# Where two weight loads stand among GpSimd's casts, and how the last output block is cut

## The chip, the cores and the metric

The kernel runs on one core of a Trainium2 chip. A core has TensorE (PE), VectorE (DVE), ScalarE (ACT), GpSimd (POOL) and SyncE (SP), each with its own instruction queue in order, and sixteen DMA engines that all queues share. The metric is the device time of one execution in microseconds; the median of several runs counts.

## The reference

Sliding-window attention with a linear distance bias, then a feed-forward layer. B = 8 batches, H = 8 heads, S = 576 tokens, D = 64.

```python
scores = q @ k.T / 8 - slope[h] * |i - j|      # only 0 <= i - j < 128, else -1e9
attn   = softmax(scores) @ v                   # [B, H, S, D]
x      = attn.transpose(0, 2, 1, 3).reshape(4608, 512)
h      = x @ w_in                              # w_in  [512, 2048]
g      = h * clip(h + 3, 0, 6) / 6
out    = g @ w_out                             # w_out [2048, 512], out [4608, 512] fp32
```

## The kernel before

All matrix products are in bf16; q, k, v and the weights come as fp32. A group `g` is a pair of heads of one batch (NP = 4 groups in a batch, 32 in all); batch 0 is groups 0 to 3, batch 1 is groups 4 to 7. For each group PE forms the scores in two PSUM tiles, `scd` (the diagonal 128x128 blocks) and `sco` (the blocks beside the diagonal); ScalarE takes the exponential into `pd` and `po`; where no table was added to the scores, GpSimd masks them (lines 354 and 364). PE multiplies with v (`attend` in batches 0 and 1, `values` later; lines 383 and 391), DVE divides by the row sums, PE transposes the result (`back`, line 432), and it is copied into `xT`, the input of the feed-forward layer.

The feed-forward layer goes over nine blocks `nt` of 512 tokens. `moe_up(nt, ms)` is one of 16 steps for 128 columns of `w_in`: four matmuls (line 451), one activation on ScalarE (line 470), one multiplication on DVE (line 471). `moe_down(nt, step)` forms 128 rows of the output (`sub`) in four parts of four matmuls (line 483); at its end one engine copies the PSUM tile `ops` to `osb` and a DMA writes it out. For the last 128 rows of the last block, ScalarE copies the columns 0 to 255 and DVE the columns 256 to 511 of one PSUM tile, and two DMAs, on ScalarE's and on SP's queue, write 128 KB each. These units are woven between the attention steps by `fill(n)`, which takes the next `n` units of a fixed list as long as their tokens are ready. `up_begin(nt, ms, 3)` does the first three matmuls of a step ahead.

The order on every engine is the order in which the program is written: the whole kernel is in a manual schedule, so an instruction that waits holds all that stand behind it on its engine.

The weights are loaded by GpSimd's DMA queue, which casts them to bf16 on the way. `load_w_in(g)` loads the columns 512 g to 512 g + 511, so that the up steps `ms` = 4 g to 4 g + 3 need quarter g; quarter 0 is asked for earlier, between the casts of batch 0's v. `second_w_in` asks for quarter 1, with a memset ahead of it that touches one column of `w_out_sb`. `w_out_sb` serves in batch 0 as the room for `pd` and `po`, two rows of four for each of its four groups, and the touched place is the first of group 1's `pd`: the memset has to wait until PE has read it in `attend(1)`. `w_out` itself is loaded later, in `second_batch` (line 171).

q and k of batch 1 come over SP's queue into `ldbuf`, two pairs of heads at a time (`load_double`, two DMAs for each `dp` and each of k and q). `prepare_double(b, dp, copies, nms)` casts them to bf16 on GpSimd, two casts (line 227) for k and two for q; `wide_double` has PE transpose them (line 254). The v tokens of batch 1 follow on SP's queue as five DMAs (`load_tokens(1, "v")`, pieces of 256 bytes), then q and k of batch 2 (`load_double(2, ...)`). `cast_tokens(1, "v")` casts v on GpSimd (lines 187 and 190). Behind it on GpSimd stand two masks, the four loads of `w_out`, two masks, and the casts of batch 2's k and q, whose first result PE transposes at line 242.

The part of `first_batch` that the change touches:

```python
        prepare_double(1, 0, (P, P), early=second_w_in)   # between the first two casts
        ...
        prepare_double(1, 1, (P, P))
        load_w_in(2)
        load_w_in(3)
```

Of the kernel before, what the change touches and what calls it, by code (L numbers as in the profile page):

```python
# [10 lines left out]
FP32 = mybir.dt.float32  # L11
# [7 lines left out]
def kernel(  # L19
# [9 lines left out]
    nc = tc.nc  # L29
    B, H, S, D = q.shape  # L30
    d_model, d_ff = moe_w_in.shape
# [11 lines left out]
    n_ms = d_ff // 128  # L43
    n_ks = d_model // 128
    NT = 512
    n_nt = Ntok // NT
# [8 lines left out]
    w_out_sb = perm.tile([128, n_ms, d_model], BF16)  # L55
# [14 lines left out]
    opool = ctx.enter_context(tc.tile_pool(name="opool", bufs=4))  # L70
# [79 lines left out]
    def warm_up(n):  # L150
        w = ps_av.tile([128, 128], FP32, tag="av", name="w")
        for _ in range(n):
            nc.tensor.matmul(w, lhsT=ident, rhs=ident, start=True, stop=True)  # L153
# [11 lines left out]
    def load_w_in(g):  # L165
        nc.gpsimd.dma_start(
            out=w_in_sb[:, :, ts(g, 512)],
            in_=moe_w_in[:, ts(g, 512)].rearrange("(k p) f -> p k f", p=128))
# [6 lines left out]
    def second_w_in():  # L175
        nc.gpsimd.memset(w_out_sb[:, 4, 0:1], 0.0)
        load_w_in(1)
# [26 lines left out]
    def prepare(g, copies):  # L204
        for nm, copy in zip("qk", copies):
            pr = prs.tile([128, RT * D], BF16, tag=f"pr{nm}", name="pr",
                          padded_shape=[128, 2 * RT * D])
            copy(out=pr, in_=runs[nm][:, g % NP, :])
            st[g, nm] = pr

    def transposes(g, copies):
        b, hp = divmod(g, NP)
        for nm, dst, copy in (("q", qTb[b % 2], copies[0]), ("k", kTb[b % 2], copies[1])):
            src = st.pop((g, nm))
            tp = ps_h.tile([128, RT, RP], BF16, tag="h", name="tp", padded_shape=[128, 16, 64])
            for t in range(RT):
                for e in range(2):
                    r = slice(e * D, (e + 1) * D)
                    nc.tensor.transpose(tp[r, t, :], src[r, ts(t, D)], ident[r, r])  # L219
            copy(out=dst[:, hp, :, :].rearrange("p j c -> p (j c)")[:, 0:S].rearrange(  # L220
                "p (a t) -> p a t", t=RT), in_=tp.rearrange("p t a -> p a t"))

    def prepare_double(b, dp, copies, nms="kq", early=None):
        for nm, copy in zip(nms, copies):
            pr = prs.tile([128, RT, 2 * D], BF16, tag=f"pr{nm}", name="pr2")
            for e in range(2):
                copy(out=pr[:, :, ts(e, D)],  # L227
                     in_=ldbuf["qk".index(nm)][:, ds((2 * dp + e) * RT * D, RT * D)].rearrange(
                         "p (t d) -> p t d", t=RT))
                if early and (nm, e) == (nms[0], 0):  # L230
                    early()
            st[b, dp, nm] = pr

    BANKS = {"h": ps_h, "av": ps_av, "o": ps_o}
# [31 lines left out]
    def tables_diag(g):  # L266
        scd = ps_sc.tile([128, 2, 512], FP32, tag="sc", name="scd")
        st[g, "scd"] = scd
        for e in range(2 if diag_tabled(g) else 0):
            t = tab[:, 2 * (g % NP) + e, 1:2, :]  # L270
            nc.tensor.matmul(scd[:, e, :].rearrange("p (j c) -> p j c", j=4), lhsT=ident,
                             rhs=t.to_broadcast([128, 4, 128]), start=True, stop=False)
# [12 lines left out]
    def scores_diag(g):  # L285
        rooms(g)
        b, hp = divmod(g, NP)
        qT, kT = qTb[b % 2][:, hp, :, :], kTb[b % 2][:, hp, :, :]
        first = not diag_tabled(g)
        if (g, "scd") not in st:  # L290
            tables_diag(g)
        scd = st[g, "scd"]
        for j in range(4):
            for e in range(2):
                r = slice(e * D, (e + 1) * D)
                nc.tensor.matmul(scd[:, e, ts(j, 128)], lhsT=kT[r, j, :],  # L296
                                 rhs=qT[r, j, :], start=first, stop=first or j == 3)

    def tables_off(g):
        hp = g % NP  # L300
        sco = ps_sc.tile([128, 2, 512], FP32, tag="sc", name="sco")
        st[g, "sco"] = sco
        if full(g):
            for e in range(2):
                h = 2 * hp + e
                t = tab[:, h, 0:1, :]
                nc.tensor.matmul(sco[:, e, 128:512].rearrange("p (j c) -> p j c", j=3),
                                 lhsT=ident, rhs=t.to_broadcast([128, 3, 128]),
                                 start=True, stop=False)
                nc.tensor.matmul(sco[:, e, 0:128].rearrange("p (s c) -> p s c", s=2),  # L310
                                 lhsT=ident, rhs=tab[:, h, :, 0:64], start=False, stop=False)
# [26 lines left out]
    def exp_full(g):  # L338
        for e in range(2):
            exp_diag(g, e)  # L340
        exp_off_full(g)
# [98 lines left out]
    gts, ops = {}, {}  # L440
# [21 lines left out]
    def moe_up(nt, ms):  # L462
        gts[nt] = gbuf[nt % 2]
        hps, n = begun.pop((nt, ms), (None, 0))
        if hps is None:
# [5 lines left out]
        nc.vector.scalar_tensor_tensor(out=gts[nt][:, ms, :], in0=r6, scalar=1.0, in1=hps,  # L471
                                       op0=ALU.min, op1=ALU.mult)

    def moe_down(nt, step):
        sub, part = divmod(step, 4)
        if part == 0:
            if nt == n_nt - 1 and sub in (1, 2) or nt == 1 and sub == 0:
                ops[nt, sub] = ps_h.tile([128, d_model], FP32, tag="h", name="ops")
            else:
                ops[nt, sub] = ps_o.tile([128, d_model], FP32, tag="o", name="ops")  # L480
        for i in range(4):
            ms = part * 4 + i
            nc.tensor.matmul(ops[nt, sub], lhsT=gts[nt][:, ms, ts(sub, 128)],  # L483
                             rhs=w_out_sb[:, ms, :], start=(ms == 0), stop=(ms == n_ms - 1))
        if part == 3:
            rows = ds(nt * NT + sub * 128, 128)
            osb = opool.tile([128, d_model], FP32, tag="osb", name="osb")
            if nt == n_nt - 1 and sub == 3:
                nc.scalar.copy(out=osb[:, 0:256], in_=ops[nt, sub][:, 0:256])
                nc.vector.tensor_copy(out=osb[:, 256:512], in_=ops[nt, sub][:, 256:512])  # L490
                nc.scalar.dma_start(out=out[rows, 0:256], in_=osb[:, 0:256])
                nc.sync.dma_start(out=out[rows, 256:512], in_=osb[:, 256:512])
                return
            if nt == n_nt - 1 and sub % 2 == 0:
                nc.scalar.copy(out=osb, in_=ops[nt, sub])
                nc.scalar.dma_start(out=out[rows, :], in_=osb)
            else:
                nc.vector.tensor_copy(out=osb, in_=ops[nt, sub])  # L498
                nc.sync.dma_start(out=out[rows, :], in_=osb)
# [21 lines left out]
    V, P, A = nc.vector.tensor_copy, nc.gpsimd.tensor_copy, nc.scalar.copy  # L521
# [24 lines left out]
    def first_batch():  # L546
        prepare(0, (V, A))
        warm_up(20)
        tables_diag(0)
        tables_off(0)  # L550
        warm_up(10)
        transposes(0, (V, A))
        scores_diag(0)
        prepare(1, (P, V))
        transposes(1, (V, V))
        scores_off(0)
        exp_full(0)
        scores_diag(1)
        prepare(2, (P, P))
        tables_off(1)  # L560
        transposes(2, (V, V))
        scores_off(1)
        exp_full(1)
        scores_diag(2)
        prepare(3, (P, V))
        tables_off(2)
        transposes(3, (V, V))
        scores_off(2)
        exp_full(2)
        scores_diag(3)  # L570
        scores_off(3)
        exp_full(3)
        cast_v(0, 0, V)
        cast_v(0, 1, P)
        load_w_in(0)
        cast_v(0, 2, V)
        cast_v(0, 3, V)
        cast_v(0, 4, P)
        for dp in range(2):
            for nm in "kq":  # L580
                load_double(1, dp, nm, nc.sync)
        load_tokens(1, "v")
        attend(0)
        attend(1)
        back(0)
        attend(2)
        back(1)
        prepare_double(1, 0, (P, P), early=second_w_in)
        attend(3)
        back(2)  # L590
        up_begin(0, 0, 3)
        back(3)
        wide_double(1, 0, "q", V)
        prepare_double(1, 1, (P, P))
        load_w_in(2)
        load_w_in(3)
        for dp in range(2):
            for nm in "kq":
                load_double(2, dp, nm, nc.sync)
        up_begin(0, 1, 3)  # L600
        done[0] = NP
        fill(1)
        wide_double(1, 0, "k", A)
        fill(2)
# [147 lines left out]
```

## Time and profile before

| | |
|---|---|
| median of 3 runs | 324.28 us (324.0 to 325.56) |
| the profiled execution | 324.27 us, span 322.6 us |
| granted TensorE clock | 0.999 |
| PE busy | 311.8 us, 97% of the span |
| ACT, DVE, POOL busy | 61%, 54%, 43% |
| up-projection matmuls (line 451) | 640 instructions, 144.9 us |
| down-projection matmuls (line 483) | 576 instructions, 141.3 us |
| loads of `w_in` | 4 issues, 7.1 to 9.9 us to landing |

The span runs from the first to the last instruction; the execution's own time is 1.67 us longer. Matmuls are pipelined and their ends are modelled, so the starts of neighbouring matmuls tell more than their durations. A line of the timeline or the waits names the engine, the source line, the tile written and the tile read. "q0" is the DMA queue that GpSimd fills, "q1" that of SP.

### The profile page before, as it was taken

How to read it: one execution, taken by the hardware profiler on the slowest of the kernel's cores; microseconds unless marked ns; L12 is line 12 of the kernel's file. 1: busy time of each engine (PE TensorE's matmuls, PEld its weight loads, DVE VectorE, ACT ScalarE, POOL GpSimd, SP SyncE). 2: the span in 40 equal slices, each digit the busy share in tenths (PEclk: the TensorE clock that was granted, in tenths of full speed). 3: DMA queues.
4: the chain of work that ended last, by engine and by line, in shares of the span. 5: the costliest groups of instructions: out<-in, count | busy, mean ns of one | idle time of the engine just before them, and what ended most of it. 6: DMA issues, size and time to landing. Idle time of an engine off the chain costs nothing.

```text
span 322.6 us, 7017 instructions
## 1 busy us (share of the span) xinstructions
PE 311.8 (97%) x2722; PEld 166.1 (52%) x2722; DVE 173.1 (54%) x338; ACT 195.2 (61%) x334; POOL 140.1 (43%) x249
## 2 busy tenths in 40 slices
PE   7889999999999999999999999999999999999995
PEld 6565465554554454555677654455444444444442
DVE  6767574554356555555555555555556455455500
ACT  4749976877777666766676667666764344244301
POOL 7465592693593767356745665463331000000000
PEclk9999999999999999999999999999999999999999
DMA  7999999999999999999999999932112100000111
GB/s 279 223 323 201 273 243 201 231 232 200 202 255 177 219 214 184 200 223 205 187 191 200 225 190 199 220 84 79 26 50 84 56 34 35 33 33 33 67 65 65
DMA packets 131425, 51.90 MB, mean 161 GB/s; under 512 B 118976, under 2 KB 123328, under 8 KB 131392
## 3 DMA queue, kind: packets, MB, share of 16 engines
q1 hardware_dynamic: 126160, 45.43, 65.7%
q0 software_dynamic: 4224, 4.19, 8.2%
q10 hardware_dynamic: 1008, 1.84, 1.5%
q8 instruction: 21, 0.34, 0.4%
q14 instruction: 12, 0.10, 0.1%
HBM read 36.70 MB, written 9.44 MB: 143 GB/s over the span
## 4 chain that ended last, share of the span: by engine, by line
PE 82%; DMA 7%; ACT 4%; DVE 2%; POOL 2%; issue 1%; POOLq 0%
PE ops L483 37%; PE hps L451 33%; DMA ldbuf<-in_q_dram 3%; PE scd L296 3%; DMA qTb<-tbuf 2%; DMA w_in_sb<-in_moe_w_in_dram 2%; PE av L391 2%; PE av L383 2%; ACT r L470 2%; PE sco L328 1%; PE w L153 1%; ACT kTb L244 1%; DVE kTb L220 1%; PE tp L219 1%; POOL tbuf L194 1%
## 5 line engine op out<-in xcount | busy, mean ns | idle before, releaser
L471 DVE SCALAR_TENSOR_TENSOR gbuf<-r,hps 128x512 bf16<-128x512 f32 x144 | 98.7, 687 | 103.1 <-ACT r L470 101.6
L470 ACT ACTIVATE r<-hps,bias 128x512 f32<-128x512 f32 x144 | 99.0, 689 | 90.1 <-PE hps L451 89.7
L451 PE MATMUL hps<-xT,w_in_sb 128*128 128x512 bf16 (+1 forms) x640 | 144.9, 358 | 1.3 <-DMA w_in_sb<-in_moe_w_in_dram 0.4
L483 PE MATMUL ops<-w_out_sb,gbuf 128*128 128x512 bf16 x576 | 141.3, 379 | 0.0
L451 PEld LDWEIGHTS <-w_in_sb 128*128 128x128 bf16 x640 | 58.9, 98 | 54.7 <-DMA w_in_sb<-in_moe_w_in_dram 1.4
L483 PEld LDWEIGHTS <-gbuf 128*128 128x128 bf16 x576 | 53.8, 98 | 59.1
L354 POOL TENSOR_SCALAR_AFFINE_SELECT pd<-pd 128x512 bf16<-128x512 bf16 x48 | 29.5, 631 | 34.6 <-ACT pd L351 34.6
L364 POOL TENSOR_SCALAR_AFFINE_SELECT po<-po 128x512 bf16<-128x512 bf16 x48 | 30.1, 632 | 32.2 <-ACT po L361 32.1
L351 ACT ACTIVATE pd<-scd,bias_d 128x512 bf16<-128x512 f32 x48 | 31.5, 684 | 5.0 <-PE scd L296 3.6
L194 POOL CAST tbuf<-ldbuf 128x512 bf16<-128x512 f32 (+1 forms) x45 | 25.5, 611 | 18.7 <-DMA qTb<-tbuf 10.4
L498 DVE COPY osb<-ops 128x512 f32<-128x512 f32 x33 | 22.7, 687 | 20.3 <-PE ops L483 20.3
L361 ACT ACTIVATE po<-sco,bias_o 128x512 bf16<-128x512 f32 x48 | 33.0, 688 | 0.0
L402 DVE TENSOR_TENSOR avs<-av,rc 128x384 bf16<-128x384 f32 (+1 forms) x48 | 23.6, 491 | 1.6
L391 PEld LDWEIGHTS <-pd 128*128 128x128 bf16 x192 | 14.4, 97 | 8.3 <-POOL tbuf L194 0.5
L383 PE MATMUL av<-vbuf,po 128*128 128x65 bf16 x192 | 18.1, 193 | 0.5 <-POOL po L364 0.5
L391 PE MATMUL av<-vbuf,pd 128*128 128x65 bf16 x192 | 17.6, 194 | 0.3 <-ACT kTb L244 0.3
L187 POOL CAST vbuf<-ldbuf 128x1024 bf16<-128x1024 f32 x14 | 14.3, 1041 | 4.5 <-DMA ldbuf<-in_v_dram 4.5
L383 PEld LDWEIGHTS <-po 128*128 128x128 bf16 x192 | 14.4, 98 | 3.7 <-POOL po L364 0.7
L367 ACT ACTIVATE p4buf<-sco,bias_d 128x64 bf16<-128x64 f32 x48 | 15.5, 323 | 0.0
L227 POOL CAST pr<-ldbuf 128x576 bf16<-128x576 f32 x20 | 12.8, 667 | 4.1 <-DMA ldbuf<-in_q_dram 2.1
L296 PE MATMUL scd<-qTb,kTb 64*128 64x128 bf16 x256 | 12.7, 219 | 1.7 <-DVE kTb L220 0.9
L296 PEld LDWEIGHTS <-kTb 64*128 64x128 bf16 x256 | 7.2, 94 | 13.4 <-issue 9.7
(94 smaller groups left out, 208.9 us busy)
## 6 DMA issues: line engine op xcount, KB each, us to landing
out_dram<-osb SPq DMA_DIRECT2D x33, 256.0 KB, 2.4
ldbuf<-in_v_dram SPq DMA_DIRECT2D x32, 256.0 KB, 5.5
ldbuf<-in_q_dram SPq DMA_DIRECT2D x20, 256.0 KB, 4.8
ldbuf<-in_k_dram SPq DMA_DIRECT2D x16, 256.0 KB, 4.6
ldbuf<-in_q_dram SPq DMA_DIRECT2D x12, 288.0 KB, 7.2
ldbuf<-in_k_dram SPq DMA_DIRECT2D x12, 288.0 KB, 7.0
w_in_sb<-in_moe_w_in_dram POOLq DMA_DIRECT2D x4, 512.0 KB, 8.9
w_out_sb<-in_moe_w_out_dram POOLq DMA_DIRECT2D x4, 512.0 KB, 11.2
```

The source lines that it names most:

```text
L194: nc.gpsimd.tensor_copy(out=tbuf[:m, :, j, :], in_=s[:m, j, :, :].rearrange("p (i e) d -> p i (e d)", e=2))
L296: nc.tensor.matmul(scd[:, e, ts(j, 128)], lhsT=kT[r, j, :], rhs=qT[r, j, :], start=first, stop=first or j == 3)
L351: nc.scalar.activation(out=pd[:, e, :, :].rearrange("p j c -> p (j c)"), in_=sc[:, e, :], func=ACT.Exp, bias=bias_d[:, h:h + 1], scale=scale)
L354: nc.gpsimd.affine_select(out=pd[:, e, :, :], in_=pd[:, e, :, :], pattern=[[0, 4], [1, 128]], channel_multiplier=-1, base=0, compare_op=AL ...
L361: nc.scalar.activation(out=po[:, e, :, :].rearrange("p j c -> p (j c)"), in_=sc[:, e, :], func=ACT.Exp, bias=bias_o[:, h:h + 1], scale=scale)
L364: nc.gpsimd.affine_select(out=po[:, e, :, :], in_=po[:, e, :, :], pattern=[[0, 4], [-1, 128]], channel_multiplier=1, base=-1, compare_op=A ...
L383: nc.tensor.matmul(out_av, lhsT=po[:, e, qt % 4, :], rhs=vb[:, qt - 1, h, :], start=True, stop=False)
L391: nc.tensor.matmul(out_av, lhsT=d, rhs=vb[:, qt, h, :], start=(qt == 0), stop=True)
L451: nc.tensor.matmul(hps[:, lo:hi], lhsT=w_in_sb[:, ks, ts(ms, 128)], rhs=xT[:, ks, ds(src, hi - lo)], start=(ks == 0), stop=(ks == n_ks - 1))
L470: nc.scalar.activation(out=r6, in_=hps, func=ACT.Relu, bias=bias3[:, 0:1], scale=1.0 / 6.0)
L471: nc.vector.scalar_tensor_tensor(out=gts[nt][:, ms, :], in0=r6, scalar=1.0, in1=hps, op0=ALU.min, op1=ALU.mult)
L483: nc.tensor.matmul(ops[nt, sub], lhsT=gts[nt][:, ms, ts(sub, 128)], rhs=w_out_sb[:, ms, :], start=(ms == 0), stop=(ms == n_ms - 1))
```

## The change

Three edits.

The second quarter of `w_in` is asked for ahead of the first cast of batch 1's k, where before it stood between the first and the second cast. The third quarter is asked for between the two k casts and the two q casts of the second `prepare_double` of batch 1, where before it stood behind all four, together with the fourth; the fourth keeps its place.

The last 128 rows of the output are formed in two PSUM tiles, from different pools: first 16 matmuls of 384 columns, which ScalarE copies and sends out, then 16 matmuls of 128 columns with the same 16 stationary blocks loaded again, which DVE copies and SP sends out. Before there were 16 matmuls of 512 columns and the copies were cut at column 256.

```diff
+    def last_rows(nt, sub, cut=384):
+        rows = ds(nt * NT + sub * 128, 128)
+        osb = opool.tile([128, d_model], FP32, tag="osb", name="osb")
+        for lo, hi, tag, copy, eng in ((0, cut, "o", nc.scalar.copy, nc.scalar),
+                                       (cut, d_model, "h", nc.vector.tensor_copy, nc.sync)):
+            ps = BANKS[tag].tile([128, hi - lo], FP32, tag=tag, name="ops",
+                                 padded_shape=[128, d_model])
+            for ms in range(n_ms):
+                nc.tensor.matmul(ps, lhsT=gts[nt][:, ms, ts(sub, 128)],
+                                 rhs=w_out_sb[:, ms, lo:hi],
+                                 start=(ms == 0), stop=(ms == n_ms - 1))
+            copy(out=osb[:, lo:hi], in_=ps)
+            eng.dma_start(out=out[rows, lo:hi], in_=osb[:, lo:hi])
+
     def moe_down(nt, step):
         sub, part = divmod(step, 4)
+        if nt == n_nt - 1 and sub == 3:
+            if part == 3:
+                last_rows(nt, sub)
+            return
...
-            if nt == n_nt - 1 and sub == 3:
-                nc.scalar.copy(out=osb[:, 0:256], in_=ops[nt, sub][:, 0:256])
-                nc.vector.tensor_copy(out=osb[:, 256:512], in_=ops[nt, sub][:, 256:512])
-                nc.scalar.dma_start(out=out[rows, 0:256], in_=osb[:, 0:256])
-                nc.sync.dma_start(out=out[rows, 256:512], in_=osb[:, 256:512])
-                return
...
-        prepare_double(1, 0, (P, P), early=second_w_in)
+        second_w_in()
+        prepare_double(1, 0, (P, P))
...
-        prepare_double(1, 1, (P, P))
+        prepare_double(1, 1, (P,), "k")
         load_w_in(2)
+        prepare_double(1, 1, (P,), "q")
         load_w_in(3)
```

## The prediction

> **What bounds the kernel now.** I read the page first, then who waits for whom on PE, then the timelines of POOL and PE, the DMA windows and the last microseconds.
>
> ```profile
> PE 311.8 (97%) x2722; PEld 166.1 (52%) x2722; DVE 173.1 (54%) x338; ACT 195.2 (61%) x334; POOL 140.1 (43%) x249
> PE 82%; DMA 7%; ACT 4%; DVE 2%; POOL 2%; issue 1%; POOLq 0%
> ```
>
> PE is busy for 97% of the span and is 82% of the chain that ended last. So a change that moves loads and copies can only win the few places where PE stands still. The waits of PE between 20 and 60 us, where the weights come in:
>
> ```profile
> PE hps L451 <- DMA w_in_sb<-in_moe_w_in_dram: 0.4, 1, 0.4
> PE tb L432 <- ACT xT L438: 0.4, 2, 0.2
> PE hps L451 <- DVE gbuf L471: 0.3, 1, 0.3
> ```
>
> One matmul waits for `w_in` at all, for 0.4 us. The chain shows which, and POOL's timeline shows why:
>
> ```profile
> 26.59 0.61 POOL pr L227
> 27.21 7.12 DMA w_in_sb<-in_moe_w_in_dram
> 34.38 1.05 PE hps L451 x4
> ```
>
> ```profile
> 16.76 0.67 POOL L227 CAST pr<-ldbuf 128x576 bf16<-128x576 f32 x1
> 17.78 0.10 POOL L176 MEMSET w_out_sb<- 128x1 bf16 x1 [0.35 <-PE wide L391]
> 17.82 0.74 POOL L166 DMA_DIRECT2D w_in_sb<-in_moe_w_in_dram  x1
> 19.69 0.66 POOL L227 CAST pr<-ldbuf 128x576 bf16<-128x576 f32 x1 [1.14 <-DMA ldbuf<-in_k_dram]
> 23.57 0.67 POOL L227 CAST pr<-ldbuf 128x576 bf16<-128x576 f32 x1 [0.57 <-DMA ldbuf<-in_k_dram]
> 25.10 0.67 POOL L227 CAST pr<-ldbuf 128x576 bf16<-128x576 f32 x1 [0.87 <-DMA ldbuf<-in_q_dram]
> 27.21 1.48 POOL L166 DMA_DIRECT2D w_in_sb<-in_moe_w_in_dram  x2
> ```
>
> Columns: start, duration, line, operation, and in brackets POOL's idle time before it with its releaser. The third and fourth quarter are issued at 27.21 and 27.95, behind a cast that waited for a q load. The third lands 7.1 us later, at 34.33, and up-projection step 8 starts at 34.38.
>
> **Part 1, the second quarter ahead of the first cast: nothing.** In the row above POOL had already finished the first cast (16.76 + 0.67 = 17.43) and stood idle for 0.35 us: the memset waits for PE's line 391, the first matmul of `attend(1)`, which reads the part of `w_out_sb` that the memset touches. It started at 17.52 and is not moved. So memset and issue stay at 17.78 and 17.82, whoever is queued behind them. The cast now comes after the issue: 17.82 + 0.74 = 18.56, and ends near 19.23. The next cast cannot start before its k data at 19.69, which leaves a cover of 0.46 us. Without that cover a late cast would push the three after it, and PE's transposes of q at 22.50 follow the last one (ending 22.18) by 0.3 us. PE's step 4, the first to read this quarter, started at 27.72; its PSUM buffer was freed by DVE (line 471) only at 27.67, so even an earlier landing would have been worth at most 0.05 us. I take 0.
>
> **Part 2, the third quarter between the casts of k and q.** The last k cast ends at 23.57 + 0.67 = 24.24. The issue takes 0.74 and ends at 24.98; the q cast behind it starts at 25.10 because its load lands then, so 0.12 us of cover remain. If that went, q's casts (ending 27.26) would be late by tenths; PE takes this q at 30.33, 3 us later. The fourth quarter keeps its place at 27.21. POOL's mask (line 354) behind it may start 0.7 us sooner, which is worth nothing: PE reads that tile in `attend(4)` at 41.33.
>
> When does the third quarter land? From issue to landing the four quarters took 8.0, 9.9, 7.1 and 9.8 us, so 24.24 gives 31.3 to 34.1. In the DMA windows the second quarter's packets run until about 26.4, then POOL's queue is nearly empty until 29.4. The third can use that hole. Landing by 31.5 is my value.
>
> What does PE gain? Step 8 could start as soon as the score matmuls before it are through: they start at 33.57 and the same group took 0.29 us elsewhere (29.17 to 29.46), so 33.86 instead of 34.38, 0.52 us. ScalarE takes the result; it had been idle for 0.46 us before its step at 35.45, and is then busy without a gap until 42.7. So 0.46 us is what can be passed on. I take 0.46, bounds 0 and 0.52.
>
> What does the hole cost others? It was not empty: the v tokens of batch 1, on SP's queue, ran in it alone. Each row is one microsecond (the first from 28, the pair from 30); packets, MB, share of 16 engines:
>
> ```profile
> q1 hardware_dynamic: 894, 0.23, 99.9%
> ```
>
> ```profile
> q0 software_dynamic: 164, 0.17, 103.1%
> q1 hardware_dynamic: 61, 0.02, 11.4%
> ```
>
> Beside `w_in` (q0) the v tokens (q1) fall from some 860 packets in a microsecond to between 60 and 240. They now lose the hole and get it back after 33.3 instead of 36.3, three microseconds sooner. The engines do the same work in another order, and the last v packets stay near 36.9. SP is held in its v issues meanwhile, and the q and k loads of batch 2 behind them start later; their casts begin at 44.98, some 7 us after those loads run. The last v landings gate POOL:
>
> ```profile
> 38.12 1.04 POOL L187 CAST vbuf<-ldbuf 128x1024 bf16<-128x1024 f32 x1 [3.78 <-DMA ldbuf<-in_v_dram]
> 44.98 2.50 POOL L227 CAST pr<-ldbuf 128x576 bf16<-128x576 f32 x4
> ```
>
> From 38.12 POOL has no gap until 49.94. The first two casts at 44.98 end at 46.26; PE transposes their result at 46.43. With PE 0.46 earlier it would want it at 45.97 and wait 0.29. A little behind, PE stood still for 0.36 us at 47.62 for ScalarE (line 438), whose chain is shifted too, so that wait is absorbed.
>
> **Part 3, the last block.** PE's last matmul ended at 318.82, and then:
>
> ```profile
> 318.85 0.37 ACT L489 COPY osb<-ops 128x256 f32<-128x256 f32 x1 [2.87 <-PE ops L483]
> 319.25 0.42 DVE L490 COPY osb<-ops 128x256 f32<-128x256 f32 x1 [6.62 <-ACT osb L489]
> 319.70 0.33 SPq L492 DMA_DIRECT2D out_dram<-osb  x1
> ```
>
> The two copies of one PSUM tile run one after the other: 0.88 us from PE's end to the last issue. Now there are two PSUM tiles, so DVE's copy waits for PE alone. The first copy (384 columns; between 0.37 for 256 and 0.585 for 512, so 0.48) and its issue run beside the short matmuls. DVE's copy of 128 columns: 0.687 for 512, 0.423 for 256, so 0.29. From PE's end: 0.03 + 0.29 + 0.03 = 0.35, saving 0.53. The last transfer halves to 64 KB; it landed in 1.8 us, and I count nothing for that (bound: 0.1 better).
>
> PE pays: 16 matmuls of 512 columns took 16 x 0.216 = 3.45. Those of 384 (line 307) are 0.16 to 0.17 apart: 16 x 0.163 = 2.61. Those of 128 with a weight load each (line 254) start at 23.87 nine at a time, and the next operation at 24.37, 0.056 each: 0.89. Sum 3.50, a loss of 0.05. Net gain 0.48, bounds 0.1 (were the short ones paced by their weight loads, 98 ns by line 483: 1.57 in place of 0.89, which eats 0.68 and turns it into a loss of 0.2) and 0.6. I take the row of line 254 because it has the same load and the same width; the loss of 0.2 stays in the range.
>
> The Trainium skill, TensorE: Matmul & The Clock Gate, section Back-to-back issue gap, speaks against this cut: it gives about 81 ns for each 128-column matmul in a stream of loads and matmuls, and 131 ns for one of 512 columns. By it the short ones would take 1.30 us and the gain of the last block would shrink to about 0.1. The trace has 56 and 216 ns.
>
> **The sum.** The profiled execution took 324.27 us (span 322.6 and 1.67 around it), 0.01 from the median of 324.28. 324.27 - 0 - 0.46 - 0.48 = 323.3. That is 0.3% less; 0.5% (1.62 us) is about what a measurement of this kernel can tell from no change, so the likeliest verdict is within.
>
> **Rivals.**
> - *Only the tail lands.* PE's 0.46 is taken back before 60 us, at the transposes of 46.43 or at the waits on ScalarE at 47.6 and 48.3. For it: POOL's chain from 38.12 is not moved by PE. Against: the 0.36 at 47.62. 324.27 - 0.48 = 323.8. Chance 0.17.
> - *The v tokens come late.* If the two quarters hold them back altogether until 33.3, the some 4,040 v packets left at 26.4 need 4.7 us from there, to 38.0 instead of 36.9. POOL's chain starts 1.1 later, PE waits for k at 46.43; all but 0.1 is paid: 324.3. The change is slower than before once v is later than about 1.0 us, and by over 0.5% from 2.6 us (SP's held issues leaving its queue empty would do it): 324.3 to 326. For it: 61 against 164 packets above. Against: work is only reordered. Chance 0.2, of it 0.14 beyond 0.5%.
> - *More comes free.* The hole near 29.4, where the engines idled 0.4 us, closes, v lands earlier and POOL's chain with it, and the gains stand at their upper bounds: 324.27 - 0.52 - 0.6 - 0.4 = 322.75; the scatter of the runs (324.0 to 325.56 before) decides whether it passes 0.5% (322.66). Chance 0.16, of it 0.12 beyond.
> - That part 1 does not do what it says is in the forecast.
>
> The forecast has 0.47. Scatter puts 0.03 of it past 0.5% faster and 0.01 of the tail's rival past 0.5% slower; so faster 0.15, slower 0.15, same 0.70. The range of eight in ten goes from 322.5 (half of the free gain's case lies below) to 325.0 (a little over half of the late v tokens' case above).
>
> **What would show it.** Right: memset still near 17.8 behind an idle POOL; third quarter issued near 24.3, no PE wait on `w_in` at step 8; v cast near 38; DVE's last copy 0.3 us behind PE's end. Wrong: the v cast past 39, PE waiting for POOL's casts near 46, or short matmuls at 80 ns and more.

## The result, and the profile after

The changed kernel's median is 323.47 us over 22 runs (322.6 to 325.71), that of the kernel before over the 22 runs beside them 325.13 us (324.0 to 327.75). The ratio is 0.996, with a 95% interval of 0.9944 to 0.9976: some 1.3 us faster, between 0.8 and 1.8. The profiled execution took 323.38 us, span 321.7.

The front on POOL (start, duration, line, operation, idle time before it and its releaser):

```profile
17.93 0.11 POOL L176 MEMSET w_out_sb<- 128x1 bf16 x1 [1.26 <-PE wide L391]
17.97 0.74 POOL L166 DMA_DIRECT2D w_in_sb<-in_moe_w_in_dram  x1
18.71 0.68 POOL L227 CAST pr<-ldbuf 128x576 bf16<-128x576 f32 x1
21.12 1.42 POOL L227 CAST pr<-ldbuf 128x576 bf16<-128x576 f32 x2 [1.74 <-DMA ldbuf<-in_k_dram]
26.41 0.74 POOL L166 DMA_DIRECT2D w_in_sb<-in_moe_w_in_dram  x1
28.48 0.67 POOL L227 CAST pr<-ldbuf 128x576 bf16<-128x576 f32 x1 [0.39 <-DMA ldbuf<-in_q_dram]
37.95 1.04 POOL L187 CAST vbuf<-ldbuf 128x1024 bf16<-128x1024 f32 x1 [2.94 <-DMA ldbuf<-in_v_dram]
```

The memset waits for line 391 as before. The third quarter is issued at 26.41, two microseconds ahead of the last q cast; both the k and the q data came one to two microseconds later in this execution than in the first trace. GpSimd casts v in three pieces; the second v cast, at 37.95, stands where it stood (38.12). PE around steps 4 to 9 of the up projection, in the changed kernel:

```profile
27.46 1.97 PE L451 MATMUL hps<-xT,w_in_sb 128*128 128x512 bf16 x7
31.93 1.90 PE L451 MATMUL hps<-xT,w_in_sb 128*128 128x512 bf16 x8
35.83 1.04 PE L451 MATMUL hps<-xT,w_in_sb 128*128 128x512 bf16 x4
```

and in the kernel before:

```profile
31.26 1.90 PE L451 MATMUL hps<-xT,w_in_sb 128*128 128x512 bf16 x8
34.38 1.04 PE L451 MATMUL hps<-xT,w_in_sb 128*128 128x512 bf16 x4 [0.45 <-DMA w_in_sb<-in_moe_w_in_dram]
35.68 1.04 PE L451 MATMUL hps<-xT,w_in_sb 128*128 128x512 bf16 x4
```

The 8 matmuls at 31.93 are steps 6 and 7, the 4 at 35.83 are step 9. Between their starts lie 3.90 us; before, from 31.26 to 35.68, 4.42. (I measure to step 9, since the record of step 8's first matmul is missing in several traces.) The wait for the third quarter is gone. The waits of PE between 20 and 60 us show one that is new:

```profile
PE hps L451 <- DMA w_in_sb<-in_moe_w_in_dram: 0.9, 1, 0.9
PE tb L432 <- ACT xT L438: 0.4, 2, 0.2
PE tp L254 <- POOL pr L227: 0.3, 1, 0.3
```

The 0.9 us stands at 22.37, at the first matmul of the up projection, which reads quarter 0. Its load is not touched by the change, and no other of the fourteen traces has this wait: it is this execution's. The end of the changed kernel, and below it the copy of the rows before (`sub` 2) in the kernel before:

```profile
315.12 0.58 ACT L507 COPY osb<-ops 128x512 f32<-128x512 f32 x1 [6.32 <-PE ops L501]
317.72 0.48 ACT L485 COPY osb<-ops 128x384 f32<-128x384 f32 x1 [2.01 <-PE ops L482]
318.61 0.29 DVE L485 COPY osb<-ops 128x128 f32<-128x128 f32 x1 [6.25 <-PE ops L482]
318.93 0.33 SPq L486 DMA_DIRECT2D out_dram<-osb  x1
```

```profile
315.39 0.58 ACT L495 COPY osb<-ops 128x512 f32<-128x512 f32 x1 [6.32 <-PE ops L483]
```

From the copy of `sub` 2 to the last issue: 318.93 - 315.12 = 3.81 us, before 319.70 - 315.39 = 4.31. DVE's copy now waits for PE, not for ScalarE.

**Two traces are not enough.** The spans differ by 0.9 us, and one could take it for the prediction's 0.94. Only 0.50 of it is in the tail. At the first output copy the changed kernel is 0.17 *later* (60.33 against 60.16), because of the 0.9 us at 22.37. Between the output copies at 101 and 111 us it wins 0.59 (9.54 against 10.13), where GpSimd waits for a DMA transpose that the change does not touch (4.76 us against 5.35). So the front's gain was neither shown nor refuted by this pair, and the experiments had to tell.

### The profile page after: what moved, and what is told of

Read it like the earlier page. It is cut to its first block, busy times and chain, and to the rows that moved or that the text cites. A ratio compares the mean times of both kernels' runs of the same rounds, so it can differ in the third digit from the quotient of the medians.

```text
span 321.7 us, 7010 instructions
## 1 busy us (share of the span) xinstructions
PE 308.1 (96%) x2699; PEld 166.7 (52%) x2738; DVE 172.7 (54%) x338; ACT 195.1 (61%) x334; POOL 140.7 (44%) x249
## 4 chain that ended last, share of the span: by engine, by line
PE 82%; DMA 5%; ACT 4%; POOL 4%; issue 2%; DVE 2%; SPq 1%; POOLq 0%
PE ops L501 35%; PE hps L451 35%; DMA ldbuf<-in_q_dram 3%; PE scd L296 2%; DMA qTb<-tbuf 2%; PE av L391 2%; PE av L383 2%; ACT r L470 2%; PE sco L328 1%; PE ops L482 1%; ACT kTb L244 1%; PE tp L254 1%; POOL tbuf L194 1%; ACT gbuf L351 1%; SPq L98 1%
## 5 line engine op out<-in xcount | busy, mean ns | idle before, releaser
L451 PE MATMUL hps<-xT,w_in_sb 128*128 128x512 bf16 (+1 forms) x621 | 142.7, 358 | 2.3 <-DMA w_in_sb<-in_moe_w_in_dram 0.9
L501 PE MATMUL ops<-w_out_sb,gbuf 128*128 128x512 bf16 x540 | 134.2, 380 | 2.3 <-issue 1.7
L501 PEld LDWEIGHTS <-gbuf 128*128 128x128 bf16 x560 | 52.2, 98 | 57.2
L354 POOL TENSOR_SCALAR_AFFINE_SELECT pd<-pd 128x512 bf16<-128x512 bf16 x48 | 29.6, 631 | 34.5 <-ACT pd L351 34.4
```

The source lines that it names most:

```text
L354: nc.gpsimd.affine_select(out=pd[:, e, :, :], in_=pd[:, e, :, :], pattern=[[0, 4], [1, 128]], channel_multiplier=-1, base=0, compare_op=AL ...
L451: nc.tensor.matmul(hps[:, lo:hi], lhsT=w_in_sb[:, ks, ts(ms, 128)], rhs=xT[:, ks, ds(src, hi - lo)], start=(ks == 0), stop=(ks == n_ks - 1))
```

## The experiments

All edits are relative to the kernel before or to the changed one; "old place" is that of the third quarter behind the q casts, "new place" that between k and q. Each traced kernel gave one more look at the front.

**Tail alone.** Both front edits undone:

```diff
-        second_w_in()
-        prepare_double(1, 0, (P, P))
+        prepare_double(1, 0, (P, P), early=second_w_in)
...
-        prepare_double(1, 1, (P,), "k")
-        load_w_in(2)
-        prepare_double(1, 1, (P,), "q")
+        prepare_double(1, 1, (P, P))
+        load_w_in(2)
         load_w_in(3)
```

> Only the cut of the last 128 output rows is changed. My theory: the tail is worth 0.48 us by itself, 0.15% (the same in every run, since nothing in it waits for a load): from the start of the copy of sub 2 to the issue of the last transfer 3.81 us as in the changed kernel, against 4.31 before; ratio 0.9985. Rival A (the front gives nothing and the whole measured 1.3 us is the tail): ratio 0.996. Rival B (the 128-column matmuls are paced by their weight loads): 32 matmuls take over 4.1 us and the ratio is 1.000 or above.

Measured: 0.9967 (0.9951 to 0.9983), 3.82 us from the copy of `sub` 2 to the last issue. The timing is about twice what the trace shows, so it was repeated:

> The tail-only kernel once more, because its timing (0.9967, 0.9951 to 0.9983) is about twice what its trace shows (0.50 us from the copy of sub 2 to the last issue, and some 0.1 us sooner landing: 0.9982). Theory: the trace is right, ratio 0.997 to 0.9985, and both timings together hold 0.9982. Rival (the tail gains a further 0.5 us that the trace does not show, after the last instruction): ratio 0.9967 again or below, with the execution's own time less than 1.6 us above the span.

Measured: 0.9976 (0.9957 to 0.9994); 3.81 us. Both intervals hold 0.9982. The last transfer, 64 KB, landed in 1.6 to 1.7 us where 128 KB took 1.8, so the trace accounts for some 0.6 us (0.50 and 0.1). Rival B falls: the 32 matmuls took 3.49 us, not over 4.1. Rival A (the whole gain is the tail, 0.996) is not excluded by the timing, since both intervals hold 0.996 too; their middles make the tail worth 1.1 and 0.8 us. But no row shows more than the 0.6: the second traced execution took 1.7 us more than its span, as the others did. Where the rest of that timing would come from stays open.

**Third quarter alone.**

```diff
-        prepare_double(1, 1, (P, P))
+        prepare_double(1, 1, (P,), "k")
         load_w_in(2)
+        prepare_double(1, 1, (P,), "q")
         load_w_in(3)
```

> Only the third quarter of w_in stands between the k and the q casts. My theory: this edit carries the rest of the gain: no wait of PE for w_in at up step 8, 0.46 us or somewhat more on average, because in single runs the third quarter comes later than in the one profiled; ratio 0.997 to 0.9985. Rival (the front gains nothing that lasts: what PE wins at step 8 is taken back before 60 us, and the 0.6 us that the changed kernel's profile won at 103 us, at a DMA transpose, was chance): ratio 1.000, and the first down-projection matmul of the kernel near 51.8 us as before.

Measured: 0.997 (0.9946 to 0.9995). Again:

> The third-quarter-only kernel once more. From step 6 to step 9 of the up projection the five traces with the old place of the third quarter took 4.42, 4.37, 5.54, 4.59 and 5.46 us, all eight with the new place 3.90. Theory: 3.90 again, the second v cast before 38.5 us (38.1 to 40.8 with the old place), and the edit alone is worth 0.5 to 1.2 us: ratio 0.996 to 0.9985. Rival (the front gains less than the tail and is lost in the scatter): ratio 0.999 to 1.001.

Measured: 0.9987 (0.9972 to 1.0002). Steps 6 to 9 took 3.90 and 3.91 us, the second v casts came at 38.02 and 37.51. In the first timing the edit gains by itself; the second interval just includes no change. Its size lies between 0 and 1.8 us by the two intervals, near 0.7 by their middle.

**Second quarter alone.**

```diff
-        prepare_double(1, 0, (P, P), early=second_w_in)
+        second_w_in()
+        prepare_double(1, 0, (P, P))
```

> Only the second quarter is asked for ahead of the first cast of batch 1's k. My theory: nothing, ratio 1.000 (0.998 to 1.002): the memset still waits for PE's first matmul of attend(1), starts near 17.8 to 17.9 with POOL idle for about 1.2 us before it, and the cast behind it still ends before its successor's data land. Rival (part 1 is what makes the changed kernel's front start without a wait at step 4): ratio 0.998 or below, with PE's step 4 free of a wait and the issue earlier than 17.8.

Measured: 1.0009 (0.999 to 1.0028). The memset started at 18.33, after POOL had been idle for 1.93 us. Its front has the old place of the third quarter, and PE pays for it:

```profile
32.33 1.90 PE L451 MATMUL hps<-xT,w_in_sb 128*128 128x512 bf16 x8
36.57 1.04 PE L451 MATMUL hps<-xT,w_in_sb 128*128 128x512 bf16 x4 [1.58 <-DMA w_in_sb<-in_moe_w_in_dram]
```

The wait that was 0.45 in the first trace is 1.58 here: the q casts ended late, and the third quarter was issued at 29.14 instead of 27.21. The v tokens were late as well, though not for the second v cast, which stands at 38.09, but for the third:

```profile
41.60 0.61 POOL L190 CAST vbuf<-ldbuf 64x512 bf16<-64x512 f32 x1 [2.47 <-DMA ldbuf<-in_v_dram]
```

**The changed kernel without part 1, and the changed kernel again.** In the first, `second_w_in` goes back between the two k casts:

```diff
-        second_w_in()
-        prepare_double(1, 0, (P, P))
+        prepare_double(1, 0, (P, P), early=second_w_in)
```

> The changed kernel with part 1 undone: the second quarter again between the two k casts, the third between k and q, the new tail. Theory 1 (part 1 is worth nothing or costs up to 0.3 us, the other two add up): ratio 0.994 to 0.996, at or below the changed kernel's repeat in this call; step 8 follows step 6 in 2.6 us without a wait for w_in. Theory 2 (part 1 helps where the k data come late, because the memset and the issue then no longer stand behind the cast: 18.9 and 19.4 us in the two kernels with the old order, 17.9 and 18.3 in those with the new one): PE waits 0.3 to 0.8 us at step 4 for the second quarter, and the ratio is 0.001 to 0.002 above the changed kernel's.

> The changed kernel once more, for the comparison on one chip and a second trace of it. Theory: ratio 0.995 to 0.997; no wait of PE of more than 0.2 us at step 8; 3.81 us from the copy of sub 2 to the last issue; from 101 to 111 us it takes about 9.5 us between the two output copies there, as in all traces but that of before (10.1), which would show that this 0.6 us is no part of the change. Rival (the 0.6 us at 103 us belongs to the change): traces without the third quarter's move show 10.1 there; the tail-only kernel already showed 9.7.

Measured on one chip: 0.9969 (0.9942 to 0.9995) without part 1, 0.9965 (0.9939 to 0.9991) with it. Part 1 is worth nothing that can be measured here. The wait of 0.3 to 0.8 us at step 4 that Theory 2 expected without part 1 is not in that trace. But Theory 2 has the mechanism half right. In the old order the first cast can wait for its k data, and then the memset stands behind it. POOL in the first third-quarter-alone trace:

```profile
18.76 0.67 POOL L227 CAST pr<-ldbuf 128x576 bf16<-128x576 f32 x1 [2.57 <-DMA ldbuf<-in_k_dram]
19.37 0.11 POOL L176 MEMSET w_out_sb<- 128x1 bf16 x1
```

There PE then waited 0.75 us for the second quarter at step 4. In the old order the memset started between 17.78 and 19.39 in seven traces; in the new one between 17.93 and 18.76 in six, with POOL idle for `attend(1)` each time. The edit takes away that late tail, but waits for the second quarter at step 4 remain: 0.62 and 0.75 us in two of the seven old ones (tail alone, third alone), 0.32 and 0.24 in two of the six new ones (second alone, third with second). It does not show in the time.

**No gate.** The changed kernel without the memset:

```diff
-        second_w_in()
+        load_w_in(1)
         prepare_double(1, 0, (P, P))
```

> The changed kernel, without the memset ahead of the second quarter, so that nothing holds its issue back but POOL's order. My theory: the memset is what sets the issue; without it the issue comes near 16.6, 1.3 us sooner, and the quarter's packets go among the k and q loads of batch 1. PE gains nothing from it, since in the kernel before step 4 was also held by DVE until 27.67; the k and q casts come later. Ratio to before 0.996 to 1.000, so the same as the changed kernel or up to 1 us worse. Rival (the gate costs time): ratio 0.993 or below.

Measured: 0.9977 (0.9953 to 1.0). The issue came at 16.14, step 4 had no wait for it, and PE waited 0.9 us for the casts of batch 1's k or q (line 254). The memset does set the issue. In this one trace the wait at step 4 is gone and one for a cast stands in its place, and the ratio is not better than that of the changed kernel.

**The third quarter with the second.**

```diff
         second_w_in()
+        load_w_in(2)
         prepare_double(1, 0, (P, P))
...
-        prepare_double(1, 1, (P,), "k")
-        load_w_in(2)
-        prepare_double(1, 1, (P,), "q")
+        prepare_double(1, 1, (P, P))
         load_w_in(3)
```

> The changed kernel with the third quarter asked for right behind the second, near 19.5 us, ahead of all casts of batch 1's k and q. It doubles what part 1 and part 2 could cost: 1 MB of weights between the loads of batch 1 and ahead of its v. Theory (step 8 has no wait any more, so an earlier third quarter brings nothing; the k and q loads already issued keep their order, v comes later): ratio 0.995 to 0.999, step 8 still 2.6 us behind step 6, the second v cast near 38 to 39 us. Rival (the late v tokens of the prediction): the v cast past 39 us, PE waiting for the casts near 46 us, ratio 0.999 to 1.003. Third possibility (even earlier is better): ratio 0.994 or below.

Measured: 0.9965 (0.9943 to 0.9987); steps 6 to 9 in 3.90 us, the second v cast at 38.29. With the third quarter asked for 4 to 7 us earlier than in the other kernels of the new place, the v tokens still were not past 39: the rival of late v tokens falls here too, and going earlier brings nothing beyond what the new place brings.

**The kernel before, against itself.**

> The kernel before once more, timed against itself. It tells what the comparison can tell: ratio 1.000 with an interval of about 0.002 on either side. Its second trace: theory (the 0.6 us lost near 103 us in the first trace was that execution's): 9.5 to 9.7 us between the output copies at 101 and 111 us; step 8 again waits for the third quarter, 0.4 to 1.6 us. Rival (the loss near 103 us belongs to the kernel before): 10.1 us again.

Measured: 1.001 (0.9989 to 1.0031). This trace was the surprise. The waits of PE between 20 and 60 us, and POOL's second v cast:

```profile
PE tp L242 <- POOL pr L227: 1.3, 1, 1.3
PE hps L451 <- DMA w_in_sb<-in_moe_w_in_dram: 0.8, 1, 0.8
```

```profile
40.60 1.04 POOL L187 CAST vbuf<-ldbuf 128x1024 bf16<-128x1024 f32 x1 [5.52 <-DMA ldbuf<-in_v_dram]
```

The mechanism that I feared from the change (v late, POOL's chain late, PE waiting at line 242 for batch 2's k) is here in the kernel *before*. Between 101 and 111 us it took 9.96, so my figure of 9.5 to 9.7 for this trace was wrong. The old place gave 9.39 to 10.13 there in five traces, the new one 9.28 to 9.69 in nine. Most of the 0.59 of the first pair was that pair's; whether a part of it belongs to the change stays open.

**All traces, by the place of the third quarter.**

| kernel | third issued | steps 6 to 9 | second v cast |
|---|---|---|---|
| old place: before | 27.21 | 4.42 | 38.12 |
| before again | 27.53 | 4.59 | 40.60 |
| second alone | 29.14 | 5.54 | 38.09 (third: 41.60) |
| tail alone | 28.32 | 4.37 | 39.17 |
| tail alone again | 28.64 | 5.46 | 40.78 |
| new place: changed | 26.41 | 3.90 | 37.95 |
| changed again | 24.39 | 3.90 | 37.36 |
| tail and third | 24.61 | 3.90 | 37.48 |
| third alone | 24.48 | 3.90 | 38.02 |
| third alone again | 24.03 | 3.91 | 37.51 |
| no gate | 26.86 | 3.90 | 37.67 |
| cut at 448, at 256 | 23.96, 24.39 | 3.90, 3.90 | 37.58, 38.23 |
| third with second | near 19.5 | 3.90 | 38.29 |

In all five traces the old place costs PE something at step 8: 0.47 to 1.64 us above 3.90, on average 0.98 (the sum of 0.52, 0.69, 1.64, 0.47 and 1.56, divided by five). In none of the nine did the new place. The second v cast comes at 39.35 on average in the old place and at 37.79 in the new; the third, the last, at 40.84 and 38.80.

**Does PE keep what it wins at step 8?** The first output copy, before and in the changed kernel:

```profile
60.16 0.68 DVE L498 COPY osb<-ops 128x512 f32<-128x512 f32 x1
60.33 0.69 DVE L510 COPY osb<-ops 128x512 f32<-128x512 f32 x1
```

From step 9 to this copy the two took 24.48 and 24.50 us. Thirteen of the fourteen traces lie between 24.48 and 24.55, whatever the place; only the second trace of the kernel before took 25.40, with its wait at line 242. So nothing of the gain is taken back before 60 us, and the rival "Only the tail lands" does not hold in the traces.

The mean of 0.98 is more than a typical execution loses, however. The five traced executions with the old place were on average 0.54 us longer than the median of their kernel, the seven timed ones with the new place 0.11 us shorter. At the copy of `sub` 2 the old place is 1.35 us later on average (316.46 against 315.12); less these 0.65, some 0.7 us are left. That is an estimate, and it agrees with the middle of the two timings of the third quarter alone.

Beside the new tail, the timings show less. Timed side by side on one chip, the second tail-alone kernel had a median of 323.45 and the third with the second 323.32; the first tail-alone kernel had 323.91 and the one without the gate 323.77 (both partners also ask for the second quarter earlier). The early third quarter then brings 0.13 and 0.14 us, uncertain by some 0.6 (an estimate from the scatter of 12 runs each). How the whole gain divides between the front and the tail is not settled.

**The cut.** At 448 and at 256 in place of 384, everything else as in the changed kernel; each was executed once, for its trace:

```diff
-    def last_rows(nt, sub, cut=384):
+    def last_rows(nt, sub, cut=448):      # and cut=256
```

> The changed kernel with the cut at 448: 16 matmuls of 448 columns, then 16 of 64. Theory (column streaming sets the pace, as for line 254): 16 x 0.19 + 16 x 0.03 = 3.5 us, DVE's copy of 64 columns 0.22 us, so the last SP issue comes 3.74 us after the copy of sub 2 (3.81 at 384). Rival (short matmuls are paced by their weight loads of 98 ns, or by an issue floor): 16 x 0.10 = 1.6 us for the short ones, 4.6 in all, and the issue comes 4.8 us after it. A third possibility: ScalarE's copy of 448 columns (0.53) and its DMA then end last.

> The changed kernel with the cut at 256, as in the kernel before, but in two PSUM tiles. It tells what comes of the second tile and what of the cut. Theory: the matmuls take the same 3.45 to 3.5 us (32 of 0.108), DVE's copy takes 0.42 instead of 0.29, so the issue comes 3.94 us after the copy of sub 2: of the 0.50 us, 0.37 come from the second tile (the copies no longer one behind the other) and 0.13 from the cut. Rival (the copies were one behind the other because of osb, not of PSUM): 4.3 us, as before.

The last rows at 448, then at 256:

```profile
315.34 0.58 ACT L507 COPY osb<-ops 128x512 f32<-128x512 f32 x1 [6.32 <-PE ops L501]
318.37 0.53 ACT L485 COPY osb<-ops 128x448 f32<-128x448 f32 x1 [2.44 <-PE ops L482]
318.84 0.22 DVE L485 COPY osb<-ops 128x64 f32<-128x64 f32 x1 [6.25 <-PE ops L482]
319.09 0.33 SPq L486 DMA_DIRECT2D out_dram<-osb  x1
```

```profile
315.25 0.58 ACT L507 COPY osb<-ops 128x512 f32<-128x512 f32 x1 [6.32 <-PE ops L501]
318.74 0.43 DVE L485 COPY osb<-ops 128x256 f32<-128x256 f32 x1 [6.26 <-PE ops L482]
319.20 0.33 SPq L486 DMA_DIRECT2D out_dram<-osb  x1
```

At 448 the issue follows 3.75 us behind the copy of `sub` 2, at 256 3.95. From 4.31 to 3.95 is the second PSUM tile (0.36), from 3.95 to 3.81 the cut (0.14), and the next step gives 0.06. With two tiles ScalarE's copy also starts earlier, as soon as its own 16 matmuls are done: at 256 it ended at 317.37, long before DVE's, so that trace cannot tell whether the old order came from the shared PSUM tile or from the shared `osb`. The one at 448 can: DVE starts at 318.84 while ScalarE's copy into the same `osb` runs to 318.90. DVE's copy starts 3.49 to 3.50 us behind that of `sub` 2 at every cut: PE needs the same time for these three splits. At 448 the 16 short matmuls take 318.84 - 318.37 = 0.47 us, 29 ns each with a weight load each: neither the 98 ns that the profile records for a load nor a floor above 29 ns paces them. ScalarE's transfer there goes out at 318.93, beside SP's, so this cut has little more to give.

## Why the prediction was right, point by point

- **The sum** (323.3 us, 0.94 us less) lies near the measured median, and the 0.94 inside the interval of the gain (0.8 to 1.8). The nearness of the absolute time is in part luck: the sum starts from 324.27, next to the median of three runs (324.28), and over 22 runs that kernel's median was 325.13. By medians the change gained 1.66, so a base 0.86 too low and a gain too small nearly cancel. The comparison was also finer than the 0.5% that the prediction supposed: a gain of 0.4% is clear of no change. The two halves of the sum differ in quality.
- **Part 3, the tail: right in the rows.** Predicted: 0.53 saved behind PE, 0.05 lost on PE, net 0.48. Measured: PE loses 0.03 (from the copy of `sub` 2 to the first copy that needs the last matmul 3.49 us, before 3.46), the net is 0.50, and the smaller transfer lands up to 0.2 us sooner, which I had bounded at 0.1 and left out. The 56 ns of line 254 held: 318.61 - 317.72 = 0.89 for 16 matmuls. The Trainium skill's 81 ns for a 128-column matmul (TensorE: Matmul & The Clock Gate, Back-to-back issue gap) would have made it 1.30 (an estimate, 16 x 81 ns). The lower bound of 0.1 does not follow from the term beside it, 0.48 - 0.68 = -0.20; it played no part. The timings of the tail alone (1.1 and 0.8 us) are above the 0.6 of the rows, which this account does not explain.
- **Part 2, the third quarter: right in its mechanism, its upper bound too low.** I took 0.46 us with an upper bound of 0.52 from the one trace, as if that wait were a constant. Over five traces it is 0.47 to 1.64, mean 0.98: the first trace shows nearly its smallest value, since POOL reached the issue at 27.21 there and up to 29.14 elsewhere. The upper bound of 0.52 was the wrong step; the issue follows the last q data, whose cast started anywhere in 2 us, and the wait depends on the issue, on a landing some 7 to 8 us behind it, and on how late PE itself is (tail alone: issued at 28.32, but PE reached step 6 only at 32.27, and 0.47 were left). For the typical execution 0.46 may still have been near: the timings of the edit alone give 1.0 and 0.4 us, and do not tell 0.46 from 0.98.
- **The third's landing.** "By 31.5" was too early: in the changed kernel's trace it was issued at 26.41, where I had 24.24, and landed 6.5 us later, at 32.9, since the k and q data were late. It was in time for step 8 (34.5) all the same. In six other traces of the new place the issue was near the forecast (23.96 to 24.61).
- **The v tokens: the rival had the wrong sign.** I argued that the work is only reordered and left the v cast near 38. It is on average 1.6 us earlier in the new place, the last v cast 2.0, and late v occurs in the old (past 41 us for the last cast in three of five traces). The rival "more comes free" named the direction (v earlier, POOL's chain with it) at 0.4 us. But the earlier v was worth time in one trace alone: before again lost 0.9 us between step 9 and the first output copy. In the two others with late v PE was itself late by the wait at step 8, and lost nothing more up to there. What makes v late in the old place I did not isolate: the third and fourth quarter go out back to back there, behind the q casts, and in two of five traces the second v cast waited more than 5 us.
- **Part 1: right in effect, wrong in its premise.** That the first cast is done and POOL stands idle before the memset held in two of the seven traces of the old order. In four others the cast waited for its k data, and in three of them it ended at 18.4 to 19.5 and the memset followed at once. The time does not show it (0.9969 and 0.9965).
- **The part gains** add up within their intervals only: the tail by timing 0.9967 and 0.9976, the third quarter 0.997 and 0.9987, the whole 0.996 and 0.9965. Finer than that the timings cannot tell.

## What to carry to other kernels

A wait that ends with a load's landing differs from execution to execution, and one trace shows one draw (here 0.47 to 1.64 us in five): before pricing such a wait as a constant, look at how near its releaser stood to other late loads, and take further traces where that is possible. Then compare each traced execution with the median of its kernel: here the two with the longest waits were also longer than usual, by 0.6 and 1.7 us. Where GpSimd both issues loads and casts, an issue that stands behind a cast inherits the lateness of that cast's data; here, moving the issue ahead of it cost nothing that the traces show. At the end of this kernel, two PSUM tiles in place of one let the first copy run beside the last matmuls, and that gave more (0.36 us) than the choice of the cut (0.14).

## What the runs showed of the hardware

- A matmul of 64 columns with a weight load of 128x128 each ran every 29 ns, one of 128 columns every 56 ns, one of 384 every 163 ns (2.60 us for 16): nearly in proportion to the columns, and for the short ones below the 98 ns that the profile records for a load.
- In the first trace the v tokens, in pieces of 256 bytes, ran at 825 to 894 packets in a microsecond alone (26 to 29 us) and at 61 to 239 beside the `w_in` loads (30 to 36 us); yet with the weights asked for sooner the last v cast came at 38.5 to 39.3 us, against 39.1 to 41.8.
- Between two traces of the same program the casts that wait for the k, q and v loads of batch 1 started up to 2.5 us apart (v in the kernel before: 38.12 and 40.60), at a granted clock of 0.998 to 1.0 in every trace.
